# Staggered start addresses for the split weights, and one pass in bank order, in a gated attention and token-MLP kernel

## The chip, the cores and the metric

The kernel runs on one core of a Trainium2 chip. The metric is the device time of one execution in microseconds (us). An engine is written as the profile writes it: PE is TensorE's matrix multiply, PEld its weight load, ACT ScalarE, DVE VectorE, POOL GpSimd, SP SyncE, whose queue issues nearly all DMAs here.

## The reference

One input `x` of 2048 tokens by 512 channels goes through two branches, which a gate mixes:

```python
x = A_x
g = _sigmoid((x * gate_w).sum(-1, keepdims=True))
a = _A_ref(x, A_wqkv, A_wo)               # softmax attention, 32 heads of 16 channels
b = _B_ref(x, B_w1, B_b1, B_w2, B_b2)     # MLP over the tokens
return g * a + (1 - g) * b
```

The second branch is the one that the change touches:

```python
h = _layernorm(x, axis=-1)                       # (B, S, D)
u = jnp.einsum("bsd,sf->bdf", h, w1) + b1        # (B, D, F), F = 1792
u = _gelu(u)
y = jnp.einsum("bdf,fs->bds", u, w2) + b2        # (B, D, S)
```

## The kernel before

Every matrix product of the linear layers is made from two halves of each operand: `hi` is the operand cast to the type fp32r, `lo` the rest (helper `split`, L81 to L83: a copy that casts, then a subtraction). A product of two operands is three matmuls: hi by hi, hi by lo, lo by hi.

The stages follow one another on PE: the V projection with transposes of `x` (until some 52 us), the K and Q projections (until 144.8 us), the first MLP layer (until 297.2 us), 28 matmuls of the second layer (L857), and then the attention, into which the rest of the second layer and the output projection are woven (L989 beside the scores of L868).

**The first layer** (loop from L462, matmuls at L429). It makes `u` as 14 blocks of 128 rows by 512 columns. `order` (L128) has four passes: f0 = 0, 512 and 1024 with four blocks each, f0 = 1536 with two. Each block of a pass adds up in a PSUM bank of its own (`ps`, from eight banks `acc`). A pass walks over the 16 chunks `c` of 128 tokens. For each chunk `weight()` gives one pair `hi`, `lo` (128 by 512, or 256 in the last pass), and `layer` (L425) makes 12 matmuls (6 in the last pass): for one bank after another, the three matmuls (`wh`, `h_hi`), (`wh`, `h_lo`), (`wl`, `h_hi`). The 128-column slices of the weights are the stationary operand, which PEld loads ahead of each matmul; `h_hi[c]` and `h_lo[c]`, 512 columns wide, are the moving operand.

**The weights' buffers** (pool `wk`, L115). `load_weight` (L138) brings a block to `w_raw` (four buffers) through SP's queue. `split_weight` (L151) casts it to `w_hi` on ACT and writes `w_lo` on POOL; during attention DVE casts. Both have three buffers, taken in turn. The same buffers serve the second layer (`second_layer`), where they are again the stationary operand and `u_hi`, `u_lo` are the moving one.

**GELU** (L434). Each block of `u` goes through a chain of DVE and ACT steps. For the passes f0 = 0 and f0 = 1536 (`in_order`, L464), DVE, ACT and POOL keep the order that is written: the chain of the blocks of the pass before is dealt out over the chunks there.

**Where things lie.** A pool's tiles lie end to end along each of the 128 partitions. Pools on the left grow upwards, those with `side="right"` downwards from the top. Small tiles named `pad` (32, 160 and 224 bytes) stand between them. In the program of the kernel before, the starts of the operands, as remainders of 256 bytes, are:

| tile | start in bytes | remainder |
|---|---|---|
| `h_hi`, `h_lo` (moving, first layer; left) | 52448, 68832, 87776, 104160 | 224 |
| `w_hi` (three buffers; right) | 217056, 219104, 221152 | 224 |
| `w_lo` (three buffers; right) | 223200, 225248, 227296 | 224 |
| `w_raw` (four buffers; right) | 208864 and up | 224 |
| `xt_hi`, `xt_lo`, `wc_hi`, `wc_lo` (K and Q projections; right) | 143328, 176096, 112608, 118752 and up | 224 |
| `u_hi`, `u_lo` (moving, second layer; right) | 151520, 180192 | 224 |
| `wv_hi`, `wv_lo` (V projection; right) | 82400, 84448 and up | 224 |
| `ks`, `qs` (scores; left) | 87264, 103648 and up | 224 |
| `wo_hi`, `wo_lo` (output projection, moving; left) | 52448, 60640 | 224 |
| `o_hi2`, `o_lo2`, `o_hi3`, `o_lo3` (output projection, stationary, second half of the rows; pool `end`) | 173984, 178080, 210848, 214944 | 160 |
| `hi`, `lo`, `wq0`, `wq1` (last pair of heads, L1069; pool `end`) | 223136, 225184, 190368, 194464 | 160 |

The right side ends at byte 229344. The highest tile of the left side at the time of `u` is `pt`, which ends at 151040.

Of the kernel before, what the change touches and what calls it, by code (L numbers as in the profile page):

```python
# [11 lines left out]
F32R = mybir.dt.float32r  # L12
# [10 lines left out]
P = 128  # L23
# [5 lines left out]
NS = S // P  # L29
ND = D // P  # L30
NF = F // P
NB = 512
# [43 lines left out]
def gated_mix(ctx: ExitStack, tc: tile.TileContext, a_x, a_wqkv, a_wo, b_w1, b_b1, b_w2, b_b2, gate_w, out):  # L76
    nc = tc.nc
    xf, of = (t.rearrange("b s d -> (b s) d") for t in (a_x, out))

    def split(hi, lo, src, copy, sub):  # L80

        copy(hi, src)  # L82
        return sub(lo, src, hi.bitcast(F32), ALU.subtract)  # L83
# [33 lines left out]
    wk = wk_ctx.enter_context(tc.tile_pool(name="wk", bufs=3, side="right"))  # L117

    def bank():
        return acc.tile([P, NB], F32, name="acc")  # L120
# [7 lines left out]
    order = {f0: [(c + (NS // 2 if f0 + NB >= F else 0)) % NS for c in range(NS)] for f0 in range(0, F, NB)}  # L128
# [22 lines left out]
    def split_weight(copy=None, sub=None):  # L151
        if loaded:
            raw = loaded.pop(0)
            hi = wk.tile([P, NB], F32R, name="w_hi")[:, : raw.shape[1]]
            lo = wk.tile([P, NB], F32R, name="w_lo")[:, : raw.shape[1]]
            subs.append(split(hi, lo, raw, copy or nc.scalar.copy, sub or nc.gpsimd.tensor_tensor))
            ready.append((hi, lo))

    def weight():
        load_weight()  # L160
        split_weight()
        return ready.pop(0)
# [17 lines left out]
    with tc.tile_pool(name="vp", bufs=1, side="right") as pool:  # L180
# [118 lines left out]
        for t in range(2, NS):  # L299
# [9 lines left out]
            ps = bank()  # L309
# [22 lines left out]
    h_hi, h_lo = {}, {}  # L332
# [9 lines left out]
    def ln_load(ln, c, bufs=3):  # L342
        xs[c] = ln.tile([P, D], F32, name="x", bufs=bufs)
        nc.sync.dma_start(xs[c], xf[c * P : (c + 1) * P, :])

    def ln_rows(ln, c):
        hf = ln.tile([P, D], F32, name="hf", bufs=2)
        nc.vector.tensor_scalar(hf, xs[c], mv[:, c, 0:1], rs[:, c : c + 1], ALU.subtract, ALU.mult)
        split(h_hi[c], h_lo[c], hf, nc.scalar.copy, nc.vector.tensor_tensor)
# [5 lines left out]
    with tc.tile_pool(name="ln0", bufs=3, side="right") as ln:  # L355

        def project(w, n):
            ps = bank()
            cols = slice(n * NB, (n + 1) * NB)
            hi, lo = w  # L360
            products(ps, [((hi[:, k, :], lo[:, k, :]), (xt_hi[:, k, cols], xt_lo[:, k, cols])) for k in range(ND)])
            return ps
# [11 lines left out]
        for b in range(ND):  # L374
# [3 lines left out]
            for n in range(NQ):  # L378
                ps = project(wk_b, n)
# [4 lines left out]
            for n in range(NQ):  # L384
                ps = project(wq_b, n)
# [4 lines left out]
                if n % 2 == 0:  # L390
                    c = 2 * b + n // 2
# [13 lines left out]
    def bring_most():  # L405
        nc.sync.dma_start(most_d, most)
        nc.sync.dma_start(most_row, most_d.rearrange("p b -> (p b)")[None, :])

    def least_shifts():

        far = bd.tile([1, H], F32, name="far", bufs=1)
        heads = far.rearrange("o (h b) -> o h b", b=ND)
        nc.vector.tensor_reduce(heads, most_row.rearrange("o (h d b) -> o h b d", d=DH, b=ND), axis=AX.X, op=ALU.add)
        nc.vector.tensor_scalar(far, far, BOUND_LIMIT, None, ALU.is_gt)
        ff = bd.tile([1, 1], F32, name="ff", bufs=1)
        nc.vector.tensor_reduce(ff, far, axis=AX.X, op=ALU.add)
        nc.vector.tensor_copy(flag, ff)
# [4 lines left out]
    u_hi = u_pool.tile([P, NF, D], F32R, name="u_hi")  # L422
    u_lo = u_pool.tile([P, NF, D], F32R, name="u_lo")

    def layer(ps, hi, lo, rhs, first, last):  # L425
        for i, p in enumerate(ps):
            wh, wl = hi[:, i * P : (i + 1) * P], lo[:, i * P : (i + 1) * P]
            for k, (a, b) in enumerate(((wh, rhs[0]), (wh, rhs[1]), (wl, rhs[0]))):
                nc.tensor.matmul(p, a, b, start=first and k == 0, stop=last and k == 2)  # L429

    with tc.tile_pool(name="ln1", bufs=3, side="right") as ln, tc.tile_pool(name="gl", bufs=2, side="right") as gl:

        def gelu(ps, fb):

            u = gl.tile([P, D], F32, name="gu")
            s = gl.tile([P, D], F32, name="gs")
            hi, lo = u_hi[:, fb, :], u_lo[:, fb, :]
            nc.vector.tensor_scalar_add(u, ps, b1[:, fb : fb + 1])
            yield
            nc.scalar.activation(s, u, AF.Square)  # L440
            yield
            nc.vector.tensor_scalar(s, s, GELU_A, 1.0, ALU.mult, ALU.add)
            nc.vector.tensor_mul(s, s, u)
            yield
            nc.scalar.activation(s, s, AF.Tanh, scale=GELU_C)
            yield
            nc.vector.scalar_tensor_tensor(u, s, 1.0, u, ALU.add, ALU.mult)
            yield
            nc.scalar.copy(hi, u)
            yield  # L450
            nc.vector.tensor_tensor(lo, u, hi.bitcast(F32), ALU.subtract)
            yield

        beside = {mybir.EngineType.Activation, mybir.EngineType.DVE, mybir.EngineType.Pool}
        for c in range(AHEAD):
            ln_load(ln, NH + c, AHEAD + 1)


        STEPS = 7
        gelus = []  # L460
        for f0, cs in order.items():
            n = min(NB, F - f0) // P  # L462
            ps = [bank() for _ in range(n)]
            in_order = f0 == 0 or f0 + NB >= F  # L464
            if not in_order:
                for step in gelus:
                    list(step)
                gelus = []
            with tc.manual_schedule(engines=beside) if in_order else ExitStack():
                for at, c in enumerate(cs):  # L470
                    hi, lo = weight()

                    if f0 == 0 and AHEAD < c <= NH:
                        ln_load(ln, NH + c - 1, AHEAD + 1)
                    if f0 == 0 and AHEAD < c <= NH + AHEAD:
                        ln_rows(ln, NH + c - AHEAD - 1)
                    layer(ps, hi, lo, (h_hi[c], h_lo[c]), at == 0, at == NS - 1)
                    if f0 == 0 and c == 0:
                        bring_most()
                    if f0 == 0 and c == NH + 4:  # L480
                        least_shifts()
                    for i, step in enumerate(gelus):
                        if 0 <= at - i // 2 * STEPS - i % 2 < STEPS:
                            next(step)
            gelus = [gelu(ps[i], f0 // P + i) for i in range(n)]
        for step in gelus:
            list(step)
# [76 lines left out]
    def second_layer(t):  # L564

        box = []

        def step(fc, k):
            if fc == 0 and k == 0:
                box.append(ps_dn.tile([P, D], F32, name="dn"))  # L570
            if fc % 4 == 0 and k == 0:
                load_weight()
                box.append(ready.pop(0))
            at = slice(fc % 4 * P, (fc % 4 + 1) * P)
            hi, lo = (w[:, at] for w in box[-1])
            a, b = ((hi, u_hi), (hi, u_lo), (lo, u_hi))[k]
            last = fc == NF - 1 and k == 2
            return box[0], a, b[:, fc, :], fc == 0 and k == 0, last, (lambda: second_out(t, box[0])) if last else None

        return [(step, fc, k) for fc in range(NF) for k in range(3)]  # L580
# [115 lines left out]
    def put(steps, at, sizes):  # L696
        for n in sizes:
            dense[at] = [steps.pop(0) for _ in range(n)]
            at += 1
        assert not steps  # L700
        return at
# [4 lines left out]
    def put_outputs(tiles, n, m, at):  # L706
        for t in tiles:
            steps, load = project(t, n, m)
            call(at - (2 if m > 6 else 1), load)
            at = put(steps, at, [m - n])  # L710
        return at
# [6 lines left out]
    first, at = steps[:28], put(steps[28:], 0, [8, 6])  # L718
    for t in range(1, NS):
        at = put(second_layer(t), at, [8, 6] * 3 if t in (7, 14, 15) else [6] * 7)  # L720
        if t == 7:
            call(at - 7, fetch_o, 0, 0)
            call(at - 3, fetch_o, 0, 1)
            at = put_outputs(range(NH), 0, 6, at)
# [3 lines left out]
    done, at = at, put_outputs(range(NH), 6, 12, at)  # L728
    at = put_outputs(range(NH, NS), 0, EARLY, at)
# [119 lines left out]
    with tc.manual_schedule(engines=engines):  # L849
# [3 lines left out]
        for n, (step, *args) in enumerate(first):  # L853
            if n and n % 12 == 0:
                split_weight(nc.vector.tensor_copy, nc.vector.tensor_tensor)
            ps, a, b, start, stop, done = step(*args)
# [84 lines left out]
        for grp in range(NG):  # L941
            at = [0, 0]
            for ph in range(2 * TWOS):
# [53 lines left out]
                for n in range(N_S - len(beside)):  # L997
                    i = (n + second + 1) % 2
# [24 lines left out]
        turned, whole, hi, lo = ([x[:, i * QC : (i + 1) * QC] for i in range(2)] for x in tiles)  # L1023
# [80 lines left out]
    with tc.If(far_off != 0):  # L1104
        with (
# [6 lines left out]
            for b in range(ND):  # L1112
                with tc.For_i(0, P // DH, 1) as hi:
# [7 lines left out]
                    for t in range(NS):  # L1121
# [7 lines left out]
                        p = pool.tile([P, S], F32, name="p", bufs=1)  # L1129
# [4 lines left out]
                        for n in range(NQ):  # L1134
                            tp = ps_t.tile([P, NB // P, P], F32, name="tp")
                            for i in range(NB // P):
                                c = n * (NB // P) + i
# [3 lines left out]
                            for i in range(NB // P):  # L1141
                                c = n * (NB // P) + i
# [38 lines left out]
```

## Time and profile before

| | |
|---|---|
| time, median of 3 runs | 1278.18 us (1278.14 to 1278.26) |
| span of the profiled execution | 1276.0 us |
| mean granted TensorE clock in it | 0.999 |

The profile has for each engine its busy time, for each group of instructions its count, mean duration and the wait before it, and a chain of work that ended last, which can be listed in order of time. PE's matmuls overlap: one is shown as 0.39 us long, while the next begins some 0.23 us after it. The cost of a matmul in a dense row is therefore the distance between starts and not its duration. A piece of the chain such as "144.85 152.32 PE acc L429 x672" begins at 144.85 us, is 152.32 us long, and holds 672 matmuls that follow without a gap. The time outside the span (some 2.2 us) belongs to the run and not to the kernel's instructions.

### The profile page before, as it was taken

How to read it: one execution, taken by the hardware profiler on the slowest of the kernel's cores; microseconds unless marked ns; L12 is line 12 of the kernel's file. 1: busy time of each engine (PE TensorE's matmuls, PEld its weight loads, DVE VectorE, ACT ScalarE, POOL GpSimd, SP SyncE). 2: the span in 40 equal slices, each digit the busy share in tenths (PEclk: the TensorE clock that was granted, in tenths of full speed). 3: DMA queues.
4: the chain of work that ended last, by engine and by line, in shares of the span. 5: the costliest groups of instructions: out<-in, count | busy, mean ns of one | idle time of the engine just before them, and what ended most of it. 6: DMA issues, size and time to landing. Idle time of an engine off the chain costs nothing.

```text
span 1276.0 us, 33051 instructions
## 1 busy us (share of the span) xinstructions
PE 1266.6 (99%) x13278; PEld 801.2 (63%) x13278; DVE 719.3 (56%) x1329; ACT 1071.9 (84%) x1484; POOL 210.8 (17%) x435
## 2 busy tenths in 40 slices
PE   9999999999999999999999999999999999999998
PEld 7888888886555555555555555555555555555555
DVE  5675363528776766666634346676666662325425
ACT  3444343437999999999999999999999999999994
POOL 0210144454111111111110011111111111100000
PEclk9999999999999999999999999999999999999999
DMA  4497743328443333433555533333343345446721
GB/s 133 141 304 274 241 122 99 99 71 166 84 93 59 74 76 70 79 70 76 116 107 115 129 77 69 69 72 76 68 78 72 74 82 109 98 88 198 149 62 70
DMA packets 94641, 137.37 MB, mean 108 GB/s; under 512 B 16313, under 2 KB 55375, under 8 KB 91408
## 3 DMA queue, kind: packets, MB, share of 16 engines
q1 hardware_dynamic: 93904, 134.14, 44.8%
q8 instruction: 106, 1.74, 0.6%
q10 hardware_dynamic: 576, 1.05, 0.2%
q14 instruction: 55, 0.45, 0.1%
HBM read 99.10 MB, written 36.03 MB: 106 GB/s over the span
## 4 chain that ended last, share of the span: by engine, by line
PE 99%; DMA 0%; ACT 0%; SPq 0%; DVE 0%; issue 0%
PE s L826 37%; PE s L868 34%; PE acc L429 12%; PE acc L90 10%; PE dn L989 4%; PE pa L1060 1%; PE acc L201 1%; PE dn L857 0%; PE acc L268 0%; DMA x<-in_A_x_dram 0%; ACT pt L891 0%; PE pa L1069 0%; SPq L193 0%; DVE base L1082 0%; SPq L186 0%
## 5 line engine op out<-in xcount | busy, mean ns | idle before, releaser
L891 ACT ACTIVATE pt<-s 128x512 f32<-128x512 f32 (+1 forms) x1259 | 943.5, 962 | 10.0 <-PE s L868 4.3
L868 PE MATMUL s<-qs,ks 64*128 64x512 f32 x2048 | 493.9, 404 | 0.8 <-POOL token L993 0.5
L826 PE MATMUL s<-pt,v 128*17 128x256 f32 x8024 | 482.6, 381 | 0.0
L868 PEld LDWEIGHTS s<-qs,ks 64*128 64x128 f32 x2048 | 325.4, 184 | 168.7 <-ACT pt L891 91.0
L846 DVE TENSOR_TENSOR ot<-s,ot 128x256 f32<-128x256 f32 (+2 forms) x427 | 190.4, 447 | 348.9 <-PE s L826 271.6
L826 PEld LDWEIGHTS s<-pt,v 128*17 128x17 f32 x8024 | 210.4, 97 | 232.2 <-ACT pt L891 84.2
L989 PE MATMUL dn<-u_hi,w_hi 64*128 64x512 f32 x428 | 186.4, 436 | 0.0
L83 POOL TENSOR_TENSOR w_lo<-w_raw,w_hi 128x512 fp32r<-128x512 f32 (+1 forms) x126 | 149.7, 1189 | 167.3 <-ACT w_hi L82 107.3
L989 PE MATMUL dn<-u_lo,w_hi 64*128 64x512 f32 x430 | 169.8, 395 | 0.0
L989 PE MATMUL dn<-u_hi,w_lo 64*128 64x512 f32 x430 | 169.2, 394 | 0.0
L993 POOL MEMSET token<- 1x1 f32 x256 | 26.2, 102 | 779.4 <-PE dn L989 711.8
L913 DVE SCALAR_TENSOR_TENSOR row<-row,o_hi 128x512 f32<-128x512 f32 x168 | 116.6, 694 | 4.9
L82 ACT CAST w_hi<-w_raw 128x512 fp32r<-128x512 f32 (+1 forms) x67 | 38.1, 569 | 79.4 <-PE acc L429 58.9
L429 PE MATMUL acc<-h_hi,w_hi 128*128 128x512 f32 x224 | 87.1, 389 | 0.0
L429 PE MATMUL acc<-h_lo,w_hi 128*128 128x512 f32 x224 | 87.1, 389 | 0.0
L429 PE MATMUL acc<-h_hi,w_lo 128*128 128x512 f32 x224 | 87.1, 389 | 0.0
L989 PEld LDWEIGHTS dn<-u_hi,w_lo 64*128 64x128 f32 x430 | 79.3, 184 | 1.3
L989 PEld LDWEIGHTS dn<-u_lo,w_hi 64*128 64x128 f32 x430 | 79.4, 185 | 0.4
L989 PEld LDWEIGHTS dn<-u_hi,w_hi 64*128 64x128 f32 x428 | 78.6, 184 | 1.1
L90 PE MATMUL acc<-xt_hi,wc_hi 128*128 128x512 f32 x128 | 49.8, 389 | 0.0
L90 PE MATMUL acc<-xt_lo,wc_hi 128*128 128x512 f32 x128 | 49.8, 389 | 0.0
L90 PE MATMUL acc<-xt_hi,wc_lo 128*128 128x512 f32 x128 | 49.8, 389 | 0.0
(145 smaller groups left out, 1148.5 us busy)
## 6 DMA issues: line engine op xcount, KB each, us to landing
w_raw<-in_B_w_dram SPq DMA_DIRECT2D x96, 256.0 KB
ks<-kp SPq DMA_DIRECT2D x192, 128.0 KB
qs<-qp SPq DMA_DIRECT2D x256, 64.0 KB
qp<-pc SPq DMA_DIRECT2D x16, 768.0 KB
x<-in_A_x_dram SPq DMA_DIRECT2D x32, 256.0 KB
kp<-pc SPq DMA_DIRECT2D x16, 512.0 KB
w_raw<-in_B_w_dram SPq DMA_DIRECT2D x32, 128.0 KB
bp<-row SPq DMA_DIRECT2D x16, 256.0 KB
```

Of the source, the lines that this page charges most:

```text
L82: copy(hi, src)
L83: return sub(lo, src, hi.bitcast(F32), ALU.subtract)
L90: nc.tensor.matmul(ps, a, b, start=start and n == 0, stop=stop and n == last)
L201: nc.tensor.transpose(turns[t][:, k, :], xs[t][:, k * P : (k + 1) * P], ident)
L429: nc.tensor.matmul(p, a, b, start=first and k == 0, stop=last and k == 2)
L826: mm = nc.tensor.matmul(av[32 * j : 32 * j + VC, i * QC : (i + 1) * QC], v[:, c, g % NP * 2 + i, :], pt[:, h * QC : (h + 1) * QC], start=t ...
L846: reads(nc.vector.tensor_tensor(x, y, x, ALU.add), bank)
L868: mm = nc.tensor.matmul(banks[:, bank, :], kt[grp][rows, c * P : (c + 1) * P], qt[grp][rows, qb * NB : (qb + 1) * NB], start=True, stop=True,)
L891: act = nc.scalar.activation(dst, banks[:, at[0] : at[-1] + 1, :], AF.Exp, scale=SCALE)
L913: nc.vector.scalar_tensor_tensor(box[1], q or box[1], a, x, ALU.add, ALU.mult)
L989: mm = nc.tensor.matmul(ps, a[half], b[half], start=first and not second, stop=last and bool(second))
L993: fence = nc.gpsimd.memset(token, 0.0)
```

## The change

```diff
     def split_weight(copy=None, sub=None):
         if loaded:
             raw = loaded.pop(0)
-            hi = wk.tile([P, NB], F32R, name="w_hi")[:, : raw.shape[1]]
-            lo = wk.tile([P, NB], F32R, name="w_lo")[:, : raw.shape[1]]
+            hi = wk.tile([P, NB + 24], F32R, name="w_hi")[:, : raw.shape[1]]
+            lo = wk.tile([P, NB + 8], F32R, name="w_lo")[:, : raw.shape[1]]
...
-    def layer(ps, hi, lo, rhs, first, last):
-        for i, p in enumerate(ps):
+    def layer(ps, hi, lo, rhs, first, last, by_bank):
+        order = [(i, k) for i in range(len(ps)) for k in range(3)]
+        if by_bank:
+            order.sort(key=lambda x: x[1])
+        for i, k in order:
             wh, wl = hi[:, i * P : (i + 1) * P], lo[:, i * P : (i + 1) * P]
-            for k, (a, b) in enumerate(((wh, rhs[0]), (wh, rhs[1]), (wl, rhs[0]))):
-                nc.tensor.matmul(p, a, b, start=first and k == 0, stop=last and k == 2)
+            a, b = ((wh, rhs[0]), (wh, rhs[1]), (wl, rhs[0]))[k]
+            nc.tensor.matmul(ps[i], a, b, start=first and k == 0, stop=last and k == 2)
...
-                    layer(ps, hi, lo, (h_hi[c], h_lo[c]), at == 0, at == NS - 1)
+                    layer(ps, hi, lo, (h_hi[c], h_lo[c]), at == 0, at == NS - 1, f0 == 2 * NB)
```

A buffer of `w_hi` is 24 floats (96 bytes) wider and one of `w_lo` 8 floats (32 bytes) wider; the added columns are never written or read. A `w_hi` buffer is now 2144 bytes and a `w_lo` buffer 2080, so that those that follow it start at other remainders of 256 bytes. The pool `wk` is 3 x 96 + 3 x 32 = 384 bytes larger, and all that lies below it on the right side moves down by 384 bytes.

In the third pass alone (f0 = 1024), the 12 matmuls of a chunk come in another order: first (`wh`, `h_hi`) for the four banks in turn, then (`wh`, `h_lo`) for the four, then (`wl`, `h_hi`) for the four. No instruction is added or taken away in either edit, on any engine or queue.

## The prediction

> **What bounds the kernel now.** First the page: the span, the engines' busy time, and PE's row over the 40 slices.
>
> ```profile
> span 1276.0 us, 33051 instructions
> PE 1266.6 (99%) x13278; PEld 801.2 (63%) x13278; DVE 719.3 (56%) x1329; ACT 1071.9 (84%) x1484; POOL 210.8 (17%) x435
> PE   9999999999999999999999999999999999999998
> PEclk9999999999999999999999999999999999999999
> ```
>
> PE is busy throughout and its clock is granted in every slice, so time can only come from the distance between the starts of matmuls, or from a wait that is new. The chain of work listed in order of time shows this distance by stage:
>
> ```profile
> 16.87 2.77 PE acc L90 x12
> ...
> 52.33 92.53 PE acc L90 x408
> 144.85 152.32 PE acc L429 x672
> 297.17 6.35 PE dn L857 x28
> ```
>
> The first layer is one piece without a gap: 152.32 / 672 = 0.2267 us a matmul. The projections ahead of it have the same (92.53 / 408 = 0.2268), and so do the 28 matmuls of the second layer behind it (6.35 / 28 = 0.2268). But the twelve matmuls of one V tile, of the same size, take 2.77 / 12 = 0.2308: there PE comes from transposes, and its distances vary:
>
> ```profile
> 16.94 0.40 PE L90 MATMUL acc<-wv_lo,xt_hi 128*128 128x512 f32 x1
> 17.17 0.40 PE L90 MATMUL acc<-wv_hi,xt_lo 128*128 128x512 f32 x1
> 17.41 0.39 PE L90 MATMUL acc<-wv_hi,xt_hi 128*128 128x512 f32 x1
> 17.63 0.39 PE L90 MATMUL acc<-wv_lo,xt_hi 128*128 128x512 f32 x1
> 17.86 0.40 PE L90 MATMUL acc<-wv_hi,xt_lo 128*128 128x512 f32 x1
> ```
>
> The starts are 0.23, 0.24, 0.22 and 0.23 us apart. A matmul of this size is thus no constant: it has a loose form of 0.22 to 0.24 us and a steady form of 0.2267 us, which the long stages keep. The groups of the first layer show how steady it is:
>
> ```profile
> L429 PE MATMUL acc<-h_hi,w_hi x224: 389/389/389, 144.7 to 296.3; 128*128 128x512 f32 x112
> L429 PEld LDWEIGHTS acc<-h_lo,w_hi x224: 187/188/188, 144.7 to 296.3; 128*128 128x128 f32 x112
> ```
>
> Minimum, median and maximum are equal. The weight load (0.188 us) is shorter than the distance, so loads lie beside matmuls.
>
> **Does the address matter?** All operands of these stages, moving and stationary, start at remainder 224 of 256 bytes (front table). Two places near the end differ. In the last pair of heads (L1069) both operands lie at 160. In L1060 the stationary operand lies at 160 and the moving one at 224, 64 bytes apart:
>
> ```profile
> 1263.21 1.13 PE L1069 MATMUL pa<-wq,hi 16*128 16x512 f32 x16
> 1264.12 0.68 PE L1069 MATMUL pa<-wq,lo 16*128 16x512 f32 x8
> ...
> 1264.80 4.84 PE pa L1060 x20
> ...
> 1265.54 0.62 PE L1060 MATMUL pa<-wo_hi,o_lo 96*128 96x512 f32 x2
> ...
> 1269.24 0.39 PE L1060 MATMUL pa<-wo_hi,o_lo 96*128 96x512 f32 x1
> ```
>
> L1069 runs four small matmuls at once: 16 of them take 1264.12 - 1263.21 = 0.91 us, 0.2275 for four. For L1060, from 1265.54 to 1269.24 there are 16 distances: 3.70 / 16 = 0.2313 us. After twenty matmuls in a row L1060 is still loose, while L90 and L429, with equal remainders, hold the steady form for 1080. This is the only row of the trace that has unequal remainders in matmuls that run alone, and it is 0.0046 us dearer. It also changes bank every fourth matmul, but L429 changes bank every third and is steady, so the bank is the weaker reading.
>
> **The change, part by part.**
>
> *The offsets in the first layer.* From the end of the right side, 229344, the larger pool starts at 229344 - 4 x 2048 - 3 x 2144 - 3 x 2080 = 208480, remainder 96. Behind the four raw buffers the `w_hi` buffers have remainders 96, 192, 32 and the `w_lo` buffers 128, 160, 192 (192 comes twice: by my working five offsets and not six). `h` is on the left and stays at 224. No pair is equal any more: `w_hi` stands 128, 32 and 192 bytes below `h`, `w_lo` 96, 64 and 32. If unequal remainders cost the steady form, each of the 672 matmuls costs what L1060 or the V tile cost: 672 x (0.2313 - 0.2267) = +3.1 us, or 672 x (0.2308 - 0.2267) = +2.8 us. The bounds are from the V rows: all at 0.24 would be 672 x 0.0133 = +8.9, all at 0.22 would be 672 x -0.0067 = -4.5 us. I take +3.1, the nearest row, since it alone has the cause in it.
>
> *The same buffers in the second layer's 28 matmuls* (L857): 28 x 0.0046 = +0.1 us.
>
> *The same buffers in attention.* There each L989 matmul runs beside a score on the other half of the rows, and a stretch of scores is cut off by L826. The loose form is the rule already:
>
> ```profile
> L989 PE MATMUL dn<-u_lo,w_hi 64*128 64x512 f32 x430 | 169.8, 395 | 0.0
> ...
> 1089.63 0.43 PE s L868
> 1091.66 1.85 PE s L826 x32
> 1093.52 0.42 PE s L868
> ...
> 1210.28 0.42 PE s L868
> ...
> 1245.37 0.43 PE s L868
> PEld s L868 <- ACT pt L891: 91.0, 214, 0.6
> ```
>
> A stretch of eight scores and its L826 with second-layer matmuls (224 against 224) takes 1093.52 - 1089.63 = 3.89 us. Nine such stretches with the output projection's (160 against 224) take 1245.37 - 1210.28 = 35.09, or 3.90 each. So +0.01 us for a stretch. The second layer has some 430 x 3 / 6 = 215 stretches of six: +2.1 us if all count. But in many the wait for ACT's exponentials (last row: 214 waits of weight loads) already covers so little. I take half, +1.0 us, with 0 and +2.1 as ends. `u` moves with the pool to remainder 96, so one `w_hi` buffer of three is equal to it; the scores' operands are on the left and stay.
>
> *Everything else on the right side moves by 384 bytes.* `xt`, `wc`, `wv` and `x` move together, keep equal remainders, and L1069 at 160 (0.2275) gives no sign that the remainder itself counts: 0. The left tiles end at 151040 and `u_hi` starts at 151520 - 384 = 151136, so nothing overlaps and no new wait for a place arises.
>
> *The splits.* `w_hi` and `w_lo` are written at odd offsets, by ACT and POOL.
>
> ```profile
> L83 POOL TENSOR_TENSOR w_lo<-w_raw,w_hi 128x512 fp32r<-128x512 f32 x14 | 18.8, 1345 | 19.3 <-ACT w_hi L82 19.3
> L82 ACT CAST w_hi<-w_raw 128x512 fp32r<-128x512 f32 x15 | 9.3, 618 | 19.4 <-PE acc L429 16.8 <-POOL w_lo L83 2.1 <-issue 0.5
> ```
>
> These are of the third pass (223 to 262 us). A chunk there lasts 12 x 0.2267 = 2.72 us and needs one of each: 0.62 and 1.35 us. They stay hidden unless POOL's doubles; then 2.69 against 2.72 is still just hidden. 0.
>
> *The third pass by bank.* No matmul, load or DMA is added, and SP's and POOL's queues keep their order. L429 already goes to another bank after each third matmul at the same 0.389 us, so a bank change on each costs 0. The last read of `w_hi` comes 3 matmuls (0.68 us) earlier and the first of `w_lo` 6 matmuls (1.4 us) later, which only loosens the wait of ACT's cast for L429. The first bank is complete after matmul 9 of the last chunk, not 3, so DVE's first GELU step can start 6 x 0.2267 = 1.4 us later. What hides this is the next pass, which lasts 16 x 6 x 0.2267 = 21.8 us and doesn't read the result; without cover it would be 1.4 us, once. ACT's casts for the weights stand behind GELU's ACT steps in the written order, with two pairs of buffers ahead.
>
> *Sum:* 3.1 + 0.1 + 1.0 = +4.2 us on the profiled 1276.0, which is 1280.2 in the span. The median lies 2.2 us above that span, so 1278.2 + 4.2 = **1282.4 us**.
>
> **A rule against all this.** The steady 0.2267 us beside a load of 0.188 us is the row. The Trainium skill (TensorE: Matmul & The Clock Gate, Step-by-step: what each phase is for) says that PE reads the moving and the stationary operand through two independent ports, so that a weight load takes nothing from the running matmul. By that the offsets would be worth 0 and the sum 1278.2. The loose and steady forms of one and the same matmul speak against the rule, since only the relation to the load differs; no row so far proves it.
>
> **Rivals.**
>
> 1. *No effect, 1278.2.* The steady form may come from an uninterrupted row alone, and the first layer inherits it from L90 without a gap at 144.85. Then L1060 is loose because each tile of it changes bank or since it is short. For: V tiles with equal remainders are loose too. Against: twenty matmuls of L1060 without an end to it. Partial loss belongs here as well: below 2.5 us it can't be told from nothing (0.2%, the least that a measurement of this kernel can tell from no change). Chance 0.24.
> 2. *Faster.* If the 0.2267 holds a collision of the two reads that equal remainders cause, staggered ones avoid it. The shortest distance in the rows is 0.22 (17.41 to 17.63): 672 x -0.0067 = -4.5 us, and for the 430 x 3 / 2 = 645 distances of L989's matmuls in attention -0.01 each, -6.5 us, at most; half of both gives 1272.7. It decides from a mean below 0.2229 in the first layer (2.5 / 672 less). Against: L1060. Chance 0.13.
> 3. *The clock drops in the third pass.* If PE pauses minutely at each bank change, the clock gate may close: 192 matmuls at half speed, 192 x 0.2267 = +43.5 us, 1321.7. Against: the clock row shows no slice below 9 although scores go to another bank each time. Chance 0.02. The Trainium skill (same page, A second HAM failure mode: psum-queue depth-cycling) reports such a case with banks cycled each iteration; no row here shows it.
> 4. *The offsets collide harder than L1060's.* 0.24 throughout the first layer, +8.9 with attention's +2.1: 1289.2. Chance 0.09. The change then does more than the row that I price it by.
>
> **How the numbers follow.** The forecast has 0.52, with its own range of 1280.8 to 1284.5. Slower by over 0.2% is the forecast with rivals 3 and 4: 0.63. Same is rival 1: 0.24. Faster is rival 2: 0.13. The range for 8 in 10 takes in rival 1, the weaker half of rival 2 and most of rival 4: 1277.0 to 1288.0.
>
> **What would show it.** In the profile after: the chain's piece L429 x672 of about 155.4 us, with durations that spread from 0.38 to 0.40 in place of 389/389/389; all four passes alike, the third no different from the second; L90's 408 still 92.5 us; attention within 2 us. A piece of 152.3 us makes rival 1 right, a shorter one rival 2, a clock digit below 9 rival 3. The forecast is wrong in its reason if L429 stays steady and the loss stands elsewhere, or if one pass alone carries it.

## The result and the profile after

| | before | after |
|---|---|---|
| time, median of 7 runs each | 1278.14 us (1277.62 to 1278.26) | 1282.00 us (1281.51 to 1282.49) |
| span of the profiled execution | 1276.0 us | 1280.6 us |

The ratio is 1.0031, with a 95% interval of 1.0022 to 1.0041: slower by 3.9 us, where 4.2 us were forecast. In the changed program the helper's matmuls stand at L432 in place of L429, those of L857 at L860, the scores of L868 at L871, L826 at L829, L1060 at L1063 and L1069 at L1072.

The page after: span, busy time, and PE's row over the 40 slices.

```profile
span 1280.6 us, 33052 instructions
PE 1271.5 (99%) x13278; PEld 803.6 (63%) x13278; DVE 719.3 (56%) x1329; ACT 1072.1 (84%) x1484; POOL 210.4 (16%) x435
PE   9999999999999999999999999999999999999997
PEclk9999999999999999999999999999999999999999
```

The counts of the five engines and the clock are as before. The chain listed in order of time gives the projections ahead of the first layer and the pieces at the end; a list of the changed matmul line gives minimum, median and maximum duration of each group, with first and last start:

```profile
51.92 92.53 PE acc L90 x408
...
1259.46 3.58 PE s L829 x64
...
1269.04 4.84 PE pa L1063 x20
```

```profile
L432 PEld LDWEIGHTS acc<-h_hi,w_hi x224: 187/188/192, 144.1 to 299.6; 128*128 128x128 f32 x112
L432 PE MATMUL acc<-h_hi,w_hi x224: 387/394/404, 144.3 to 299.8; 128*128 128x512 f32 x112
L432 PE MATMUL acc<-h_lo,w_hi x224: 390/396/404, 144.5 to 300.1; 128*128 128x512 f32 x112
L432 PE MATMUL acc<-h_hi,w_lo x224: 387/394/399, 144.8 to 300.3; 128*128 128x512 f32 x112
```

The projections are unchanged to 0.01 us (92.53). In the first layer no duration is fixed any more: 387 to 404 ns where it was 389/389/389, while the loads keep their median of 188. PE's rows in order of time give where the stages begin; the bracket names what ended an idle time:

```profile
144.29 0.40 PE L432 MATMUL acc<-h_hi,w_hi 128*128 128x512 f32 x1
...
300.53 0.39 PE L860 MATMUL dn<-u_hi,w_hi 128*128 128x512 f32 x1
...
306.80 0.40 PE L860 MATMUL dn<-u_hi,w_hi 128*128 128x512 f32 x1
307.40 0.47 PE L871 MATMUL s<-qs,ks 64*128 64x512 f32 x1 [0.20 <-DMA qs<-qp]
```

And the same rows of before, with the last piece of its attention from the chain:

```profile
144.69 0.39 PE L429 MATMUL acc<-h_hi,w_hi 128*128 128x512 f32 x1
...
297.01 0.39 PE L857 MATMUL dn<-u_hi,w_hi 128*128 128x512 f32 x1
...
303.13 0.39 PE L857 MATMUL dn<-u_hi,w_hi 128*128 128x512 f32 x1
303.45 0.49 PE L868 MATMUL s<-qs,ks 64*128 64x512 f32 x1
...
1255.22 3.58 PE s L826 x64
```

From the end of the projections' piece (51.92 + 92.53 = 144.45 after, 144.85 before) and these starts:

| stretch | before, us | after, us | difference |
|---|---|---|---|
| up to the end of the projections | 144.85 | 144.45 | -0.4 |
| first layer (from its first start, 144.69 and 144.29, to the next line's) | 152.32 | 156.24 | +3.9 |
| the 28 matmuls, to the first score | 6.44 | 6.87 | +0.4, of it 0.2 a wait for `qs` |
| attention, to the last L826 piece | 951.8 | 952.1 | +0.3 |
| the rest of the span | 20.8 | 21.1 | +0.3 |

A first-layer matmul takes 156.24 / 672 = 0.2325 us in place of 0.2267. The starts of the passes are 44.63, 44.61 and 44.70 us apart, and the narrow last one takes 22.31: 0.2324, 0.2323, 0.2328 and 0.2324 a matmul. The pass in bank order is no exception. The projections' end lies anywhere from 144.19 to 144.85 us in the kernels below, so the -0.4 is no part of the change. The differences add up to the 4.6 us between the two profiled spans; the profiled run of the changed kernel was its slowest (1282.49 us), and between the medians lie 3.9.

### The profile page after: what moved, and what is told of

The parts are those of the page before. It is cut to its first block, busy times and chain, and to the rows that moved or that the text cites. A ratio compares the mean times of both kernels' runs of the same rounds, so it can differ in the third digit from the quotient of the medians.

```text
span 1280.6 us, 33052 instructions
## 1 busy us (share of the span) xinstructions
PE 1271.5 (99%) x13278; PEld 803.6 (63%) x13278; DVE 719.3 (56%) x1329; ACT 1072.1 (84%) x1484; POOL 210.4 (16%) x435
## 4 chain that ended last, share of the span: by engine, by line
PE 98%; DMA 1%; ACT 0%; DVE 0%; issue 0%; SPq 0%
PE s L829 37%; PE s L871 31%; PE acc L432 12%; PE acc L90 10%; PE dn L992 6%; PE pa L1063 1%; PE acc L201 1%; PE acc L268 0%; DMA ks<-kp 0%; DMA qs<-qp 0%; ACT pt L894 0%; PE pa L1072 0%; PE acc L245 0%; DVE base L1085 0%; ACT xt_hi L82 0%
## 5 line engine op out<-in xcount | busy, mean ns | idle before, releaser
L871 PE MATMUL s<-qs,ks 64*128 64x512 f32 x2048 | 493.9, 404 | 1.0 <-POOL token L996 0.5
L829 PE MATMUL s<-pt,v 128*17 128x256 f32 x8024 | 482.6, 381 | 0.0
L871 PEld LDWEIGHTS s<-qs,ks 64*128 64x128 f32 x2048 | 325.8, 184 | 163.7 <-ACT pt L894 91.0
L829 PEld LDWEIGHTS s<-pt,v 128*17 128x17 f32 x8024 | 210.3, 97 | 232.7 <-ACT pt L894 83.2
L432 PE MATMUL acc<-h_lo,w_hi 128*128 128x512 f32 x224 | 80.8, 395 | 0.0
L432 PE MATMUL acc<-h_hi,w_hi 128*128 128x512 f32 x224 | 80.5, 394 | 0.0
L432 PE MATMUL acc<-h_hi,w_lo 128*128 128x512 f32 x224 | 80.3, 393 | 0.0
L90 PE MATMUL acc<-xt_hi,wc_hi 128*128 128x512 f32 x128 | 49.8, 389 | 0.0
L90 PE MATMUL acc<-xt_lo,wc_hi 128*128 128x512 f32 x128 | 49.8, 389 | 0.0
L90 PE MATMUL acc<-xt_hi,wc_lo 128*128 128x512 f32 x128 | 49.8, 389 | 0.0
```

What stands on the lines that cost most here:

```text
L90: nc.tensor.matmul(ps, a, b, start=start and n == 0, stop=stop and n == last)
L432: nc.tensor.matmul(ps[i], a, b, start=first and k == 0, stop=last and k == 2)
L829: mm = nc.tensor.matmul(av[32 * j : 32 * j + VC, i * QC : (i + 1) * QC], v[:, c, g % NP * 2 + i, :], pt[:, h * QC : (h + 1) * QC], start=t ...
L871: mm = nc.tensor.matmul(banks[:, bank, :], kt[grp][rows, c * P : (c + 1) * P], qt[grp][rows, qb * NB : (qb + 1) * NB], start=True, stop=True,)
```

## The experiments

**Each edit alone, and everything moved together.** The first two take one of the two edits away; the third moves all operands by 128 bytes, so that their remainders stay equal.

```diff
 # e1_offsets, from the changed kernel: no pass in bank order
-                    layer(ps, hi, lo, (h_hi[c], h_lo[c]), at == 0, at == NS - 1, f0 == 2 * NB)
+                    layer(ps, hi, lo, (h_hi[c], h_lo[c]), at == 0, at == NS - 1, False)
 # e2_bank, from the changed kernel: buffers as before
-            hi = wk.tile([P, NB + 24], F32R, name="w_hi")[:, : raw.shape[1]]
-            lo = wk.tile([P, NB + 8], F32R, name="w_lo")[:, : raw.shape[1]]
+            hi = wk.tile([P, NB], F32R, name="w_hi")[:, : raw.shape[1]]
+            lo = wk.tile([P, NB], F32R, name="w_lo")[:, : raw.shape[1]]
 # e5_all_moved, from the kernel before
-    const.tile([P, 8], F32, name="pad")
+    const.tile([P, 40], F32, name="pad")
...
+            if not subs:
+                wk.tile([P, 32], F32, name="w_pad", bufs=1)
```

Expected of e1_offsets:

> The wider weight buffers alone; the third pass keeps the order of before. Theory A (unequal remainders of 256 bytes between the weights and h cost the first layer its steady 0.2267 us a matmul): all of the loss stays, about 1282.0 us, the first layer's 672 matmuls in 156.1 to 156.3 us, the third pass like the second (44.6 us for 192 matmuls). Rival C (the bank order has a part in it): the third pass goes back to the 43.5 us of before, 1281 us or less.

Expected of e2_bank:

> The bank order of the third pass alone; the weight buffers are as before, all remainders equal. Theory A: 1278.1 us as before, the first layer 152.3 us, every duration 389 ns. Rival C: the third pass alone leaves the steady form, 44.6 us in place of 43.5, and perhaps the fourth behind it; 1279.3 to 1279.9 us.

Expected of e5_all_moved:

> All matmul operands from the V projection to the second layer moved by 128 bytes together, to remainder 96; the pool end stays at 160, pt moves to 128. Theory A (only the distance between moving and stationary operand counts): as before, 1278.1 us, first layer 152.3 us with all durations 389 ns. Rival D (remainder 224 itself is the good place, and the 384-byte move of the right side did harm): first layer 154 to 156 us and also the K and Q projections' 408 matmuls above 92.5 us.

Measured:

| kernel | us, median | ratio to before, 95% interval | first layer, 672 matmuls |
|---|---|---|---|
| e1_offsets | 1282.13 | 1.0031 (1.0019 to 1.0043) | 156.16 |
| e2_bank | 1277.99 | 1.0001 (0.9992 to 1.0010) | 152.32 |
| e5_all_moved | 1277.93 | 0.9999 (0.9990 to 1.0009) | 152.32 |

The chain's pieces, of e1_offsets, e2_bank and e5_all_moved:

```profile
144.19 156.16 PE acc L432 x672
```

```profile
144.28 152.32 PE acc L432 x672
```

```profile
52.29 92.53 PE acc L90 x408
144.82 152.32 PE acc L431 x672
```

The offsets carry the whole loss; the bank order with equal remainders costs and gives nothing. Remainder 96 for all is as good as 224 for all, so it is the relation of the operands that counts and not their place.

**Distances one by one.** In three kernels the `h` blocks of each two neighbouring chunks start further from the weights, so that one distance holds for 24 matmuls in a row in a pass.

```diff
 # e3_sweep32; e6_sweep4 has 4 * (c // 2), e7_sweep4_high 228 to 256 by 4
-        hi_t = h_pool.tile([P, NH, D], F32R, name="h_hi")
-        lo_t = h_pool.tile([P, NH, D], F32R, name="h_lo")
+        offs = [32 * (c // 2) for c in range(16)]
+        hi_t = h_pool.tile([P, NH * D + 64], F32R, name="h_hi")
+        lo_t = h_pool.tile([P, NH * D + 64], F32R, name="h_lo")
         for i in range(NH):
-            h_hi[lo + i], h_lo[lo + i] = hi_t[:, i, :], lo_t[:, i, :]
+            at = i * D + offs[lo + i] // 4
+            h_hi[lo + i], h_lo[lo + i] = hi_t[:, at : at + D], lo_t[:, at : at + D]
```

Expected of e3_sweep32:

> The weights as before, all at 224; the h blocks of two neighbouring chunks lie 32 bytes further than those of the two chunks before (0 for chunks 0 and 1, 32 for 2 and 3, up to 224 for 14 and 15), so each distance holds for 24 matmuls in a row in a pass. Theory A (equal remainders alone are steady): chunks 0 and 1 at 0.2267, or reaching it within some 10 matmuls, the other fourteen at 0.230 to 0.234; first layer about 155.6 us, run 1281.5. Rival B (not the distance but its change from one buffer to the next breaks the steady form): every distance falls into the steady form within some 10 matmuls of its 24, first layer about 153.5 us, run 1279.5. If a distance below 0.2267 exists it shows here.

Expected of e6_sweep4:

> The h blocks of two neighbouring chunks at 0, 4, 8, 12, 16, 20, 24 and 28 bytes from the weights' remainder. If the reads meet in pieces of 32 bytes, all eight stay at 0.2267 (first layer 152.3 us); in pieces of 16 bytes, the first four do. If the distance counts to the byte, the mean goes from 0.2267 at 0 to 0.2333 at 32 in between, and a distance that is better than 0 could lie there: below 0.2267.

Expected of e7_sweep4_high:

> The same below the weights' remainder: distances of -28, -24, -20, -16, -12, -8, -4 and 0 (chunks 14 and 15). At -32 the first layer had 0.2333. In pieces of 32 bytes all but 0 are at 0.2333, first layer some 156 us; to the byte, they fall from 0.2333 to 0.2267 in between.

PE's rows of e3_sweep32 where the first three distances begin in the second pass:

```profile
188.98 0.39 PE L431 MATMUL acc<-h_hi,w_hi 128*128 128x512 f32 x1
...
194.45 0.40 PE L431 MATMUL acc<-h_hi,w_hi 128*128 128x512 f32 x1
...
200.05 0.40 PE L431 MATMUL acc<-h_hi,w_hi 128*128 128x512 f32 x1
```

Between two such starts lie 24 matmuls: (194.45 - 188.98) / 24 = 0.228 us at distance 0, (200.05 - 194.45) / 24 = 0.233 at 32. All distances of the second pass, read in the same way but from starts to the nanosecond (so 32 has 233.5, shown as 234):

| moving above stationary, bytes | mean of 24, ns |
|---|---|
| 0, 32, 64, 96, 128, 160, 192, 224 | 228, 234, 229, 234, 233, 234, 234, 233 |
| 0, 4, 8, 12, 16, 20, 24, 28 | 228, 237, 233, 229, 231, 238, 234, 227 |
| -28, -24, -20, -16, -12, -8, -4, 0 | 237, 235, 228, 227, 239, 230, 228, 227 |

At 0 the first matmuls after an unequal distance are still loose (starts 230, 236, 228, 233, 230 ns apart), then every distance is 226 or 227; the second chunk is steady throughout. At the other multiples of 32 the starts repeat a pattern (at 128: 237, 229, 237, 230) that does not end within the 24. The first layers took 156.10, 155.91 and 155.56 us in the three kernels, which ran once each (1281.31, 1281.38 and 1280.77 us). This refutes the theory that only the change from buffer to buffer hurts, and also rival 1 of the prediction: the steady form is found again within a layer, and lost at a constant unequal distance. No mean is below 0.2267, so no offset tried makes the layer faster. The distance counts in steps of 4 bytes, which I had not foreseen: 4 bytes cost more than 128, while -16 is as good as 0, and 28, -4 and -20 nearly so.

**Which of the two reads.** The two run side by side: the running matmul streams `h`, and PEld loads the next weights. One kernel puts `w_lo` alone 4 bytes below; one moves the weights in place of `h`. Both make the room by having three raw buffers in place of four.

```diff
 # e8_lo_apart, from e2_bank; w_raw has bufs=3
-            lo = wk.tile([P, NB], F32R, name="w_lo")[:, : raw.shape[1]]
+            lo = wk.tile([P, NB + 64], F32R, name="w_lo")[:, 63 : 63 + raw.shape[1]]
 # e10_weights_sweep, from the kernel before; w_raw has bufs=3
+            which, at = divmod(len(subs), NS)
+            at = at // 2
+            a, b = {0: (8 * at, 8 * at), 1: (at, at), 2: (0, 8 * at), 3: (8 * at, 0)}.get(which, (0, 0))
+            hi = wk.tile([P, NB + 64], F32R, name="w_hi")[:, a : a + raw.shape[1]]
+            lo = wk.tile([P, NB + 64], F32R, name="w_lo")[:, b : b + raw.shape[1]]
```

Expected of e8_lo_apart:

> w_hi at the remainder of h, w_lo 4 bytes below it in all its buffers (a distance that had 0.2366 at once in the sweep by 4 bytes); the third pass in bank order, so that twelve matmuls are eight with w_hi and four with w_lo; w_raw has three buffers to make room. Theory L (the running matmul is slowed by the weight load beside it, which is the next matmul's): of the twelve starts in the third pass, the steps after matmuls 8 to 11 are the slow ones, 0.235 to 0.240, and the step after 12 (beside the load of the next w_hi) is short again. Theory O (a matmul is slowed by where its own weights lie, whatever is loaded beside it): the steps after 9 to 12 are slow and the one after 8 short. In the other passes the slow step of three is the one after (wh, h_lo) by L and the one after (wl, h_hi) by O.

Expected of e10_weights_sweep:

> h stays at 224 and the weights move, within their buffers, by a step for each two chunks of a pass (w_raw has three buffers to make room). Pass 1: both halves by 0, 32, ... 224 bytes. Pass 2: both by 0, 4, ... 28 bytes. Pass 3: w_lo alone by 0, 32, ... 224. Pass 4: w_hi alone by 0, 32, ... 224. Theory A to the byte (only the distance of moving from stationary counts): pass 1 has the means of the sweep by 32 read backwards (0.2267, then 0.2333, 0.2333, 0.2345, 0.2333, 0.2333, 0.2288, 0.2333); pass 2 those of -4 to -28 (0.2278, 0.2302, 0.2385, 0.2267, 0.2270, 0.2345, 0.2370). The run with w_lo alone 4 bytes off stayed at 0.2267, which theory A does not give. Theory M (where the moving operand starts counts to the byte, where the weights start in steps of 32 bytes or more): pass 1 as by A, pass 2 all at 0.2267. Theory H (the load of w_hi alone counts, since two of three matmuls have it beside or in them): pass 3 all at 0.2267, pass 4 as pass 1. If every load counts, pass 3 loses about a third of what pass 1 loses, pass 4 two thirds.

e8_lo_apart was a miss for both theories: all 672 matmuls stayed at 0.2267 (from 144.47 to 296.79 us). `w_lo` 4 bytes below `h` is free, though `h` 4 bytes above both halves of the weights costs 10 ns. The kernel ran once, in 1279.14 us; what it lost lies behind the first layer (see below, at `qs`). The sweep of the weights (one run, 1282.67 us) gave, for each 24 matmuls (12 in the narrow pass 4):

| what moves | by bytes | mean, ns |
|---|---|---|
| both halves | 0, 32, ... 224 | 227, 233, 233, 234, 233, 234, 229, 233 |
| both halves | 0, 4, ... 28 | 227, 232, 231, 230, 234, 233, 231, 235 |
| `w_lo` alone | 0, 32, ... 224 | 227, 233, 232, 233, 231, 233, 231, 231 |
| `w_hi` alone | 0, 32, ... 224 | 227, 232, 233, 230, 233, 231, 230, 234 |

By 32 bytes the first row is the sweep of `h` read backwards: the one good unequal distance, 64 with `h` moved, is now at 192. Below 32 bytes the two starts are not interchangeable (weights at 16: 234, where -16 of `h` had 227), so theory A to the byte and theory M both fall. And one load of three is enough: over the seven distances `w_lo` alone loses about 5 ns a matmul and both halves about 6, so theory H and "a third" fall too.

The same kernel shows which matmul pays. Durations (ns, minimum/median/maximum) at two places where the distance turns from 0 to 32. First the end of the second chunk with 0 in pass 1, when the next block's `w_hi` is the first one 32 bytes away:

```profile
L432 PE MATMUL acc<-h_lo,w_hi x1: 389/389/389, 149.3 to 149.3; 128*128 128x512 f32 x1
L432 PE MATMUL acc<-h_hi,w_lo x1: 397/397/397, 149.6 to 149.6; 128*128 128x512 f32 x1
```

The matmul at 149.6 has its own weights at distance 0, and the load beside it is of those 32 away. It is the slow one. Then pass 3, where `w_hi` stays and the first displaced `w_lo` is loaded beside the second matmul of the chunk:

```profile
L432 PE MATMUL acc<-h_hi,w_hi x1: 389/389/389, 238.8 to 238.8; 128*128 128x512 f32 x1
L432 PE MATMUL acc<-h_lo,w_hi x1: 397/397/397, 239.0 to 239.0; 128*128 128x512 f32 x1
L432 PE MATMUL acc<-h_hi,w_lo x1: 389/389/389, 239.3 to 239.3; 128*128 128x512 f32 x1
```

Again the matmul that runs beside the displaced load pays, and not the one that uses it. This stays so for the seven rounds of three that follow at the same distance:

```profile
L432 PE MATMUL acc<-h_lo,w_hi x7: 400/400/400, 239.7 to 243.9; 128*128 128x512 f32 x7
L432 PE MATMUL acc<-h_hi,w_lo x7: 389/389/389, 240.0 to 244.2; 128*128 128x512 f32 x7
L432 PE MATMUL acc<-h_hi,w_hi x7: 395/395/395, 240.2 to 244.4; 128*128 128x512 f32 x7
```

The matmul beside the load of `w_lo` is the slowest (239 ns to the next start), and the one that uses `w_lo` the fastest (228). So theory O falls, and theory L holds for which matmul is hit: the one that runs beside the displaced load. But L is not all of it. The third matmul, (`wh`, `h_hi`), has its own weights and the load beside it at distance 0 and still takes 395 ns (233 to the next start). So at 32 bytes the disturbance lasts beyond the matmul that it strikes, which fits that one load of three costs nearly as much as all. How it is carried over no run shows, nor why the load of e8_lo_apart disturbs nothing.

**What attention pays.** One kernel moves all that lies below the weights by 128 bytes; `h` and the weights stay equal, and of the operands that meet in a product only `u` and the weights come apart. The other tries to gain there: `qs` above `ks` and `u` above the weights by 28 bytes.

```diff
 # e4_u_apart, from the kernel before: a tile below w_raw moves all under it
+    w_pad = wk.tile([P, 32], F32, name="pad", bufs=1)
 # e9_moving_28_above, from the kernel before; w_raw has bufs=3
+    u_hi = u_pool.tile([P, NF * D + 64], F32R, name="u_hi")[:, 7 : 7 + NF * D].rearrange("p (f d) -> p f d", d=D)
+    u_lo = u_pool.tile([P, NF * D + 64], F32R, name="u_lo")[:, 7 : 7 + NF * D].rearrange("p (f d) -> p f d", d=D)
...
+    k_bufs = [stk.tile([P, S + w], F32R, name=f"ks{i}", bufs=1)[:, 1 : 1 + S] for i, w in enumerate((64, 8))]
```

Expected of e4_u_apart:

> The weights and h stay at 224, all else on the right side moves by 128 bytes, so the second layer alone has unequal remainders (u 96 against weights 224), in the 28 matmuls and in attention. Theory A: the first layer 152.3 us as before; the 28 matmuls at 0.233, 6.5 us in place of 6.35; attention's distances at 0.231 to 0.233 with or without it, since every stretch of scores is too short for the steady form, so the whole kernel within 0.5 us of before. My priced term (+1.0 us for attention, up to +2.1): 1279.1 us or so.

Expected of e9_moving_28_above:

> A try for a faster kernel: in attention and in the second layer the moving operands (qs, u) lie 28 bytes above the stationary ones (ks, the weights), the distance that came to 0.2270 to 0.2275 after one or two loose matmuls in the sweep; h and the weights of the first layer stay equal. If a stretch of scores then reaches the steady form sooner, its five distances fall from 0.232 towards 0.227, up to 25 ns for each of the 135 stretches or so that no exponential holds up: 1274.6 to 1277 us. If the break at the start of each stretch decides alone: 1278.0 as before. The first layer stays at 152.3 us in both cases.

e4_u_apart: 1278.07 us, ratio 1.0002 (0.9992 to 1.0011). The first layer is as before, and the 28 matmuls pay in full:

```profile
144.41 152.32 PE acc L430 x672
296.74 6.53 PE dn L858 x28
```

6.53 / 28 = 0.2332. Attention pays nothing that the run time can tell. There are two reasons. The first is that its distances did not grow: the five that follow the first of each stretch of eight scores, in the roughly 245 of 254 stretches where all five lie between 200 and 250 ns, have a mean of about 232 ns before and 231.5 both here and in the changed kernel. The second is in the view of busy time by stretch, here of before (PE, PEld, DVE, ACT and POOL from left, with their instructions):

```profile
310.00:1100.00 790.00, 790.00 (x9830) 450.95 (x9822) 482.37 (x905) 780.98 (x1045) 101.57 (x297) 1.00 0.43 85
```

ACT's exponentials fill 780.98 of 790 us, 98.9%. PE shows 790.00 too, but its durations overlap, and the weight loads of its scores wait for ACT 214 times (last row of the prediction's list on attention). e9_moving_28_above tells the two engines apart. Its scores came closer (the same five distances have a mean of about 230 ns), and its attention was no shorter: from the first score at 304.27 to the last L826 piece at 1256.46 it took 952.2 us, before 951.8. It came out at 1279.49 us, ratio 1.0014 (1.0005 to 1.0023), a miss for its forecast of 1278.0 or less. Of the 1.3 us between its profiled span and that of before, 0.8 are there at the first score, which waits for a DMA:

```profile
302.76 0.39 PE L857 MATMUL dn<-u_hi,w_hi 128*128 128x512 f32 x1
304.27 0.47 PE L868 MATMUL s<-qs,ks 64*128 64x512 f32 x1 [1.12 <-DMA qs<-qp]
```

The three raw buffers are the likely cause, though they were not tried alone. e8_lo_apart has them too, with `u` and `qs` as before and a first layer as before, and its first score waits in the same way; so does that of e10_weights_sweep, for 1.58 us. The chain of e8_lo_apart shows how, and its row of PE the wait:

```profile
295.42 1.30 POOL w_lo L83
...
296.74 0.37 SPq L148
...
297.15 0.46 SPq L518
...
299.97 4.13 DMA qs<-qp
```

```profile
304.24 0.46 PE L871 MATMUL s<-qs,ks 64*128 64x512 f32 x1 [0.94 <-DMA qs<-qp]
```

The load of the next weight block (L148) waits until POOL has read a raw buffer, and the transfers of `ks` and `qs` (L518) stand behind it in SP's queue. No version beats the kernel before.

## Why the prediction was right

- **The offsets in the first layer**, +3.1 forecast, +3.9 measured (156.24 against 152.32, and 156.16 with the offsets alone). The mechanism held: the durations no longer keep to 389 ns, in all passes alike, and equal remainders bring them back (e2_bank, e5_all_moved). The term was mis-sized by the row it was priced from. L1060 has its moving operand 64 bytes above the stationary one, and the sweep shows 64 to be the mildest multiple of 32 (0.229, the others 0.233 to 0.234). The change has that distance in one of six buffers, and the mean came to 0.2325, not 0.2313. L1060's own 0.2313 is above the sweep's 0.229, so the distance alone does not give its price either; its order of matmuls differs, and this was not taken further.
- **The V tile**, the second row for that term (0.2308, +2.8), has another cause. Its addresses are equal, and its eleven distances are those of a row that settles after a break: 316, 233, 236, 224, 231, 236, 228, 233, 230, 227 and 227 ns in one tile, and much the same in the next. The 408 matmuls of L90 begin with the same series and then stay at 226 or 227. That this row came near L1060's was chance. Rival 1 was right about this row, and wrong about the first layer.
- **The 28 matmuls**, +0.1 forecast; +0.2 in work (0.2332 a matmul in e4_u_apart, where the term had 0.0046 on 0.2267), and another 0.2 of waiting for `qs` in the profiled run.
- **Attention**, +1.0 forecast with 0 as the lower end; +0.3 in the two profiles, and no loss that the time of e4_u_apart could tell. The profiles of the three kernels with unequal starts there (the changed one, e1_offsets, e4_u_apart) have an attention 0.1 to 0.4 us longer than those with equal ones, so the lower end was nearly right. The price of +0.01 us a stretch rested on 3.89 against 3.90, no more than the last digit of the view, and the distances in a stretch did not grow. "I take half" then took the waits for ACT as cover for some stretches only, but ACT is 98.9% busy and bounds the attention as a whole. This and the first term were off in opposite directions by 0.8 and 0.7 us; that the sum, 1282.4, met 1282.0 so closely is luck.
- **Moving the rest of the right side, the splits, the bank order**, 0 forecast: e5_all_moved (0.9999) and e2_bank (1.0001) show it for the move and the order, and the GELU chain's later start stayed hidden. The splits made no gap either: no two starts in the changed first layer are over 0.241 us apart.
- **The rivals.** No effect falls with e3_sweep32, and with it the rule of the Trainium skill (TensorE: Matmul & The Clock Gate, Step-by-step: what each phase is for), by which a weight load takes nothing from the running matmul: here the start addresses alone decide on up to 12 ns of 239, and the measurement decides. Faster falls since no distance of the 22 tried has a mean below 0.2267. The dropped clock falls with the clock row of the page after and with e2_bank's 152.32 us. A harder collision than L1060's is part of what was seen, 0.2325 in place of 0.2313, but not 0.24 throughout. The range reached down to 1277.0 and was said to take in the weaker half of rival 2; by that rival's own working it begins at 1278.2 - 2.5 = 1275.7, so none of it was in the range, and rival 4's 1289.2 lies above its end.
- **Five offsets and not six**: the starts in the changed program are 96, 192 and 32 for `w_hi` and 128, 160 and 192 for `w_lo`.

## What to carry to other kernels

Where dense matmuls of this type and size (fp32r, 128 by 128 by 512, a weight load beside each) set the time, price them by their distances of starts and not by their durations. The spread of the durations is a quick sign: here the group whose minimum, median and maximum agree is in the steady form, and the one whose durations spread had 2.5% to gain. Give the moving operand and the stationary one the same remainder of 256 bytes by padding, and look in the built program at where they lie; a buffer widened for another reason can undo that for all that lies behind it. Price such a gain only in the stages that PE sets: in the attention beside it, with ACT at 98.9%, the same distances were worth nothing.

## What was not expected of the hardware

- The relation of the two addresses counts down to 4 bytes: 0.2267 us with `h` at the weights' remainder, 0.237 with `h` 4 bytes above it, 0.227 again with it 16 bytes below.
- It isn't the distance alone below 32 bytes: `w_lo` 4 bytes below `h` costs nothing (0.2267 in all 672), `h` 4 bytes above both halves costs 0.010 us; `h` 16 bytes below the weights costs nothing, the weights 16 bytes above `h` cost 0.007. Why is open.
- One load in three that is displaced by 32 bytes slows the matmul beside it by 11 ns of duration (400 against 389) and, by 6, also the next but one, whose own addresses are equal.
- A constant unequal distance leads to a short repeating pattern (237, 229, 237, 230 ns at 128 bytes) and an equal one to a fixed 0.2267 after some five to ten matmuls. A stage that is cut into short stretches pays the loose distances each time: a V tile of twelve matmuls reaches 226 or 227 ns in its last one to three distances, most stretches of scores not at all.
